# Two steps of the first chunk in float32 products: windowed attention with a gated MLP on one core

## The chip, the cores and the metric

The kernel runs on one core of a Trainium2 chip. The metric is the device time of one execution, in microseconds (us). A core has a matrix engine (PE, TensorE), three engines for elementwise work (ACT, ScalarE; DVE, VectorE; POOL, GpSimd), and queues that issue DMA transfers (SP's is the one used here for nearly all loads). Each engine runs its own instructions in the order in which the program lists them, and waits where an operand isn't there yet.

## The reference

Attention with a window of 128 keys and four sink keys, over 4 batches of 8 heads, 768 positions and 64 columns a head; its output, as 3072 rows of 512, goes through an MLP with 2048 hidden columns.

```
scores = q @ k.T / 8, kept where key < n_sink or 0 <= query - key < window
x = softmax(scores) @ v            # heads side by side: 3072 x 512
h = x @ w_in                       # 512 x 2048
g = h * tanh(softplus(h))
y = g @ w_out                      # 2048 x 512
```

## The kernel before, in words

The rows are cut into twelve chunks of 256. The first four, one of each batch, are worked alone (each has 8 steps of two hidden blocks of 128 columns); the other eight go in twos (16 steps of one hidden block). For each pair of heads the kernel makes scores (`att`, PE), mask and maximum (`p`, DVE), exponential (ACT), the division by the sum (L476 on DVE or L477 on ACT), transposes (L487, PE), a copy of them out of PSUM (`pth`, L292 or L295), and the product with the values (`outs`, L521), for two pairs of heads at a time in the first chunks. Its result is `x`, transposed.

A product of the MLP is made of float32r products, which keep fewer bits than float32. So each operand is split: a high part (`h`, a rounding copy) and a low part (`l`, the operand minus its high part), and a product takes three: high by high, high by low, low by high. `outs` makes the two parts of `x` (copy, then subtraction on DVE). `weights` makes the parts of a weight block: w_in and w_out come as 64-bit numbers, and s1 to s5 turn one into a float32 `z` and a rest `e`; then s7 copies the high part, s6 subtracts it from `z` and s8 adds `e`, which gives the low part. There are 32 such blocks. `step` does one hidden step: the first product into `hp` (L570), the gate in five operations on ACT and DVE (L580 to L587, in `u`), the split of `u` into `gh` and `gl`, and the second product into the accumulators (L609).

Nothing in this is ordered by hand alone. A planner gives every task a rank (the tables WI and WO for weight blocks, PAIRS for pairs of heads and `outs`), a modelled duration on each engine that may do it, and then places the tasks one after the other on the engine and at the place that it finds best; the program lists each engine's instructions in that order. Where the planner sees PE idle for over 250 ns ahead of a task with a new PSUM tile, or ahead of the first accumulators, it puts in filler products on zeros (`zero`, L771), which write nothing that is used. The tag `w` is a pool of 84 tiles of SBUF that weights, `x` and some temporaries share.

The three chunks 0 to 2 take turns, two steps of each at a time (PARTS, GROUP), and chunk 0 begins: so steps 0 and 1 of chunk 0 are the first work of the MLP, while the attention of the next chunks and the making of the weights go on.

Of the kernel before, what the change touches and what calls it, by code (L numbers as in the profile page):

```python
# [50 lines left out]
WO = -6.08, 3, 3.74, 4.03, 10.17, 6.19, 10.46, 11.32, 13.67, 15.66, 16.2, 9.12, 16.69, 18.91, 17.44, 17.26
PAIRS = (-17.41, -16.23, -9.53, -11.15, -11.81, -7.6, -8.1, -9, -4.69, -5.4, -6.04, -1.91, -3.65, -2.92, -0.58, -1.56,
         -1.55, 13.22, 16.4, 17.74, 20.65, 20.36, 19.52, 22, 21.07, 22.86, 25.11, 23.59, 26.75, 29.16, 28.34, 27.91, 30.86, 29.76, 29.47, 32.18, 32.77, 31.74, 36.46, 35.02,
         38.31, 42.01, 40.85, 41.2, 44.31, 42.85, 44.3, 47.22, 48.89, 48.43, 50.78, 51.16, 52.28, 54.74, 55, 55.47, 58.81, 60.67, 58.15, 62.94, 63.34, 61.48, 66.09, 66.95, 68.71, 71.34, 69.96, 73.76, 76.29, 76.39, 76.12, 79.36)
# [9 lines left out]
NEAR, SLOW = 2000, 4000  # L64
DUOS = (0, 1, 2, 3)
# [9 lines left out]
def f32(ap):  # L75
    return ap.bitcast(F32)
# [184 lines left out]
class Fast(Base):  # L261
# [55 lines left out]
    def weights(self, f, *ranks):  # L317
        nc, add = self.nc, self.plan.add
        deps = []
        for src, nm, r in zip((self.w_in, self.w_out), ("wi", "wo"), ranks):  # L320
# [3 lines left out]
            z.brief = e.brief = True  # L324
# [10 lines left out]
            s7 = add(r + .03, self.copy_ways(512, lambda hi=hi: hi.t, lambda z=z: f32(z.t)), [s3], [z], [hi])  # L335
# [173 lines left out]
    def outs(self, pairs, r, x, tag="att"):  # L509
# [33 lines left out]
    def step(self, st, f, rank, begins, ends, wdeps, last):  # L543
# [11 lines left out]
        eager = last and f >= st.steps - QUICK  # L555
        g1 = []
# [19 lines left out]
        u = Buf("u", [P, 2, T])  # L576
# [10 lines left out]
        e = add(r + .55, {DVE: (dve_t(N), lambda: nc.vector.scalar_tensor_tensor(u.t, u.t, 1.0, hp.t, ALU.subtract, ALU.mult))}, [a], [u, hp])  # L587
        gg = add(r + .57, self.copy_ways(N, lambda: gh.t, lambda: u.t), [e], [u], [gh])
# [105 lines left out]
    def run(self):  # L694
# [3 lines left out]
        self.wh, self.wl = ({"wi": [], "wo": []} for _ in range(2))  # L698
# [6 lines left out]
        for m, block in enumerate(blocks):  # L705
            wide = len(block) == 2
            st = SimpleNamespace(rows=[b * S + c3 * T for b, c3 in block], x_done=[{} for _ in block], part={}, kept=[], steps=NF if wide else NF // 2)
            st.x = [(Buf("w", [P, 2, T], F32R), Buf("w", [P, 2, T], F32R)) for _ in range(KT if wide else KT // 2)]
            pairs = []
            for pr in range(NPAIR):  # L710
# [7 lines left out]
                if wide or both:  # L718
                    rank, x = next(ranks), (*st.x[pr if wide else pr // 2], None, True)
                else:  # L720
                    rank, x = rank + unit * (TB + OVP + .05), (*st.x[pr // 2], pr % 2, pr % 2 == 0)
                done = self.outs(pairs, rank, x, BANKS["o"][turn] if turn < len(BANKS["o"]) else "att")
                for d in st.x_done:
                    d[pr] = done
                    if both:
                        d[pr - 1] = done
# [330 lines left out]
```

## Time and profile before

| what | value |
|---|---|
| median of 3 runs | 689.11 us (689.0 to 689.19) |
| the profiled execution's own time | 690.23 us |
| its span, first to last instruction | 688.4 us |
| PE busy | 679.2 us, 99% of the span |
| ACT busy | 525.4 us, 76% |
| DVE busy | 501.8 us, 73% |
| POOL busy | 124.4 us, 18% |
| mean granted clock of PE | 0.998 of full speed |

The profile is one execution. A share over the whole span says little by itself: the stretches differ in what limits them, and fillers and matmuls that wait a little inside the pipeline count as busy.

### The profile page before, as it was taken

The numbers are of one execution on the slowest core, as the hardware profiler recorded it, in microseconds if no ns is written. First come the engines' busy times: TensorE is split into PE (matmuls) and PEld (weight loads), VectorE is DVE, ScalarE is ACT, GpSimd is POOL, SyncE is SP. The second block draws the span as 40 slices with busy tenths as digits, with TensorE's granted clock in tenths as the row PEclk, the third lists the DMA queues.
The fourth block names the chain that finished last, engine by engine and source line by source line (L and its number), as shares of the span: only waits on it lengthen the run. The fifth ranks groups of instructions, "written<-read, shape, count | busy, mean of one in ns | idle before, by whom it ended". The sixth has DMA issues, their size and how long they took to land.

```text
span 688.4 us, 12130 instructions
## 1 busy us (share of the span) xinstructions
PE 679.2 (99%) x3980; PEld 563.6 (82%) x3980; DVE 501.8 (73%) x1442; ACT 525.4 (76%) x1223; POOL 124.4 (18%) x128
## 2 busy tenths in 40 slices
PE   8999999999999999999999999999999999999997
PEld 6778888988888888887888888887888787888885
DVE  8999999999896887666875886667677567432342
ACT  6999898987977876767876886778777676666672
POOL 1422321121104233120132131222010110000000
PEclk9999999999999999999999999999999999999999
DMA  6564343343535334041323331133340300010001
GB/s 211 175 185 124 123 139 114 116 135 98 161 97 156 88 83 134 16 110 39 95 79 91 112 86 55 40 86 95 101 109 1 86 0 25 1 62 0 1 0 67
DMA packets 49272, 60.20 MB, mean 87 GB/s; under 512 B 4912, under 2 KB 42160, under 8 KB 49200
## 3 DMA queue, kind: packets, MB, share of 16 engines
q1 hardware_dynamic: 48624, 57.69, 29.2%
q10 hardware_dynamic: 576, 1.64, 0.6%
q8 instruction: 34, 0.56, 0.3%
q14 instruction: 38, 0.31, 0.1%
HBM read 53.02 MB, written 6.29 MB: 86 GB/s over the span
## 4 chain that ended last, share of the span: by engine, by line
PE 84%; ACT 9%; DVE 5%; DMA 1%; issue 1%; ACTq 0%
PE hp L570 31%; PE acc L609 22%; PE att L609 12%; PE att L521 5%; PE att L445 5%; PE att L570 3%; ACT p L462 3%; PE att L487 2%; ACT p L477 1%; PE att L525 1%; ACT w L292 1%; ACT pth L292 1%; DMA raw<-w_in 1%; DVE u L587 1%; PE busy L1000 1%; ACT u L582 1%
## 5 line engine op out<-in xcount | busy, mean ns | idle before, releaser
L570 PE MATMUL hp<-w,w 128*128 128x256 f32 (+1 forms) x1440 | 269.8, 335 | 0.0
L570 PEld LDWEIGHTS hp<-w,w 128*128 128x128 f32 x1440 | 220.2, 189 | 28.3 <-issue 1.0
L609 PE MATMUL acc<-w,gh 128*128 128x512 f32 x500 | 137.9, 400 | 0.8 <-ACT w L292 0.5
L609 PEld LDWEIGHTS acc<-w,gh 128*128 128x128 f32 x500 | 87.7, 188 | 19.3 <-ACT gh L292 1.6
L462 ACT ACTIVATE p<-p,nm 128x136 f32<-128x136 f32 (+2 forms) x192 | 80.4, 428 | 21.2 <-DVE nm L459 20.6
L582 ACT ACTIVATE u<-u,bias 128x512 f32<-128x512 f32 x96 | 69.5, 724 | 35.0 <-DVE u L581 34.8
L587 DVE SCALAR_TENSOR_TENSOR u<-u,hp 128x512 f32<-128x512 f32 x88 | 60.1, 683 | 40.4 <-ACT u L586 37.8
L292 ACT ACTIVATE gh<-u 128x512 fp32r<-128x512 f32 x88 | 55.8, 634 | 33.7 <-DVE u L587 31.5
L580 ACT ACTIVATE u<-hp 128x512 f32<-128x512 f32 x88 | 52.5, 596 | 33.6 <-PE hp L570 32.0
L609 PE MATMUL acc<-w,gl 128*128 128x512 f32 x250 | 75.5, 394 | 0.0
L305 DVE TENSOR_TENSOR gl<-u,gh 128x512 fp32r<-128x512 f32 x72 | 51.8, 720 | 29.8 <-PE att L609 14.5
L584 ACT ACTIVATE u<-u,bias 128x512 f32<-128x512 f32 x96 | 69.6, 725 | 2.1
L303 POOL TENSOR_TENSOR w<-raw,w 64x400 fp32r<-64x400 f32 (+1 forms) x40 | 45.6, 1145 | 135.4 <-ACT w L292 50.9
L581 DVE TENSOR_SCALAR u<-u 128x512 f32<-128x512 f32 x96 | 43.0, 448 | 34.1 <-ACT u L580 33.7
L609 PE MATMUL att<-w,gh 128*128 128x512 f32 x244 | 67.5, 394 | 0.0
L586 ACT ACTIVATE u<-u 128x512 f32<-128x512 f32 x96 | 60.7, 632 | 1.9
L459 DVE CUSTOM_DVE_ANT_0 p<-att,m 128x136 f32<-128x136 f32 (+2 forms) x192 | 54.9, 313 | 3.1 <-PE att L442 1.2
L609 PEld LDWEIGHTS acc<-w,gl 128*128 128x128 f32 x250 | 46.2, 188 | 9.1 <-DVE gl L305 0.2
L457 DVE COPY_PREDICATED att<-behind,att 128x128 f32<-128x128 int32 x128 | 34.4, 292 | 25.6 <-PE att L445 25.0
L609 PEld LDWEIGHTS att<-w,gh 128*128 128x128 f32 x244 | 44.6, 188 | 8.8
L445 PEld LDWEIGHTS att<-w,w 128*128 128x128 f32 x256 | 41.1, 188 | 7.4 <-PE att L609 0.4
L445 PE MATMUL att<-w,w 128*128 128x264 f32 x256 | 45.8, 287 | 0.0
(115 smaller groups left out, 958.3 us busy)
## 6 DMA issues: line engine op xcount, KB each, us to landing
raw<-k_p SPq DMA_DIRECT2D x64, 200.0 KB, 3.4
raw<-q_p SPq DMA_DIRECT2D x64, 128.0 KB, 3.1
raw<-w_out SPq DMA_DIRECT2D x15, 512.0 KB, 3.6
raw<-w_in SPq DMA_DIRECT2D x14, 512.0 KB, 3.5
vt<-v_b SPq DMA_DIRECT2D x32, 192.0 KB, 2.6
y<-u SPq DMA_DIRECT2D x20, 256.0 KB, 2.1
ks<-k_p SPq DMA_DIRECT2D x16, 132.0 KB, 2.8
qh<-q_p SPq DMA_DIRECT2D x16, 128.0 KB, 2.9
```

Source lines behind the costliest of these rows:

```text
L292: ways[ACT] = act_t(n, psum), lambda: nc.scalar.activation(dst(), src(), AF.Copy, scale=scale or 1.0)
L305: way = dve_t(n), lambda: nc.vector.tensor_tensor(dst(), a(), b(), ALU.subtract)
L445: yield nc.tensor.matmul(st[e].t, part.t[:, e, cols], ks[e].t[:, c0:c0 + n], start=n_ == 0, stop=n_ == 1)
L459: a = add(r(.03 + .01 * e), {DVE: (dve_t(nw) + 8, lambda st=st, pv=pv, nm=nm, e=e, mask=mask, n=n, nw=nw: nc.vector.tensor_tensor_reduce(o ...
L462: a = add(r(.05 + .01 * e), {ACT: (act_t(nw, ptr=2), lambda pv=pv, nm=nm, i=i, e=e: nc.scalar.activation(pv(), pv(), AF.Exp, bias=nm.t[:, ...
L570: yield nc.tensor.matmul(out, w_.t[:, fs], x_, start=kt == 0 and n_ == 0, stop=kt == KT - 1 and n_ == 2)
L580: a = add(r + .5, {ACT: (act_t(N, True), lambda: nc.scalar.activation(u.t, hp.t, AF.Exp))}, g1, [hp], [u])
L582: sq = add(r + .52, {ACT: (act_t(N, ptr=1), lambda: nc.scalar.activation(u.t, u.t, AF.Square, bias=self.one)), DVE: shared((dve_t(N), lamb ...
L584: a = add(r + .53, {ACT: (act_t(N, ptr=1), lambda: nc.scalar.activation(u.t, u.t, AF.Ln, bias=self.half if sq.eng == ACT else self.one, sc ...
L586: a = add(r + .54, {ACT: (act_t(N), lambda: nc.scalar.activation(u.t, u.t, AF.Exp, scale=-1.0))}, [a], [u])
L587: e = add(r + .55, {DVE: (dve_t(N), lambda: nc.vector.scalar_tensor_tensor(u.t, u.t, 1.0, hp.t, ALU.subtract, ALU.mult))}, [a], [u, hp])
L609: yield nc.tensor.matmul(acc[at].t, g_.t[:, y, ts_], w_.t, start=new and n_ == 0, stop=done)
```

## The change

Chunk 0's steps 0 and 1 (`WHOLE = 2, 0, 0`) are made of single float32 products in place of three float32r products. For them `outs` copies chunk 0's result out of PSUM as a whole (`xw`), and makes the high and low part from that copy later (rank + XL), on ACT or DVE and on POOL or DVE; the later steps of chunk 0 still use the parts. Eight weight blocks (the first four of w_in and of w_out) are first completed as float32 (s6 now adds `e` to `z`), and their parts follow from the sum later (s7 copy, s8 subtraction, rank + HL). In the two steps `u` isn't split, so a copy to `gh` and a subtraction to `gl` each are gone, twice. All ranks (WI, WO, PAIRS) and some planner constants are new, and with them the order on every engine.

```diff
-PEN_C, PEN_S, PEN_N, PEN_J, PEN_Q = 50.59, 0, 2.67, 0, 3392.52
-WI = -8.52, -5.11, -2.45, -0.51, 7.12, 8.58, 9.74, 3.15, 12.1, 12.88, 13.09, 12.16, 13.77, 16.2, 17.29, 16.24
...
+PEN_C, PEN_S, PEN_N, PEN_J, PEN_Q = 50.59, 0, 9.82, 0, 2948.59
+WI = -11.75, -4.16, -4.06, -3.48, 7.63, 8.07, 7.38, 7.81, 11.31, 12.69, 13.76, 13.95, 17.17, 17.54, 17.59, 17.42
...
+WHOLE = 2, 0, 0
+XL, HL = 1.0, 1.0
...
             hi.users, lo.users = 1, 1
-            z.brief = e.brief = True
+            whole = f < 2 * max(WHOLE)
...
-            s7 = add(r + .03, self.copy_ways(512, lambda hi=hi: hi.t, lambda z=z: f32(z.t)), [s3], [z], [hi])
+            if not whole:
+                s7 = add(r + .03, self.copy_ways(512, lambda hi=hi: hi.t, lambda z=z: f32(z.t)), [s3], [z], [hi])
...
-            s6 = add(r + .06, self.sub_ways(512, lambda z=z: f32(z.t), lambda z=z: f32(z.t), lambda hi=hi: f32(hi.t)), [s7, s4], [z, hi])
-            s8 = add(r + .08, {
-                POOL: (pool_t(512), lambda z=z, e=e, lo=lo: nc.gpsimd.tensor_tensor(lo.t, f32(z.t), f32(e.t), ALU.add)),
-                DVE: shared((dve_t(512), lambda z=z, e=e, lo=lo: nc.vector.tensor_tensor(lo.t, f32(z.t), f32(e.t), ALU.add)), PEN_J)}, [s5, s6], [z, e], [lo])
+            if whole:
+                s6 = add(r + .06, {
+                    POOL: (pool_t(512), lambda z=z, e=e: nc.gpsimd.tensor_tensor(f32(z.t), f32(z.t), f32(e.t), ALU.add)),
+                    DVE: shared((dve_t(512), lambda z=z, e=e: nc.vector.tensor_tensor(f32(z.t), f32(z.t), f32(e.t), ALU.add)), PEN_J)}, [s5, s4], [z, e])
+                s7 = add(r + .07 + HL, self.copy_ways(512, lambda hi=hi: hi.t, lambda z=z: f32(z.t)), [s6], [z], [hi])
+                s8 = add(r + .08 + HL, self.sub_ways(512, lambda lo=lo: lo.t, lambda z=z: f32(z.t), lambda hi=hi: f32(hi.t)), [s7], [z, hi], [lo])
+                self.ww[nm].append((z, s6))
+            else:
+                s6 = add(r + .06, self.sub_ways(512, lambda z=z: f32(z.t), lambda z=z: f32(z.t), lambda hi=hi: f32(hi.t)), [s7, s4], [z, hi])
+                s8 = add(r + .08, {
+                    POOL: (pool_t(512), lambda z=z, e=e, lo=lo: nc.gpsimd.tensor_tensor(lo.t, f32(z.t), f32(e.t), ALU.add)),
+                    DVE: shared((dve_t(512), lambda z=z, e=e, lo=lo: nc.vector.tensor_tensor(lo.t, f32(z.t), f32(e.t), ALU.add)), PEN_J)}, [s5, s6], [z, e], [lo])
...
-        h, l, k, newx = x
+        h, l, k, newx, xw = x
         at = (lambda z: z.t) if k is None else lambda z: z.t[:, k:k + 1, :]
+        if xw:
+            w = add(r + .1, self.copy_ways(n * T, lambda: at(xw), lambda: o.t, True), [a], [o] + ([] if newx else [xw]), [xw] if newx else [])
+            a = add(r + .1 + XL, self.copy_ways(n * T, lambda: at(h), lambda: at(xw)), [w], [xw] + ([] if newx else [h]), [h] if newx else [])
+            c = add(r + .12 + XL, self.sub_ways(n * T, lambda: at(l), lambda: at(xw), lambda: f32(at(h))), [a],
+                    [xw, h] + ([] if newx else [l]), [l] if newx else [])
+            return [a, c], [w]
         a = add(r + .1, self.copy_ways(n * T, lambda: at(h), lambda: o.t, True), [a], [o] + ([] if newx else [h]), [h] if newx else [])
         c = add(r + .12, self.sub_ways(n * T, lambda: at(l), lambda: o.t, lambda: f32(at(h)), (DVE,)), [a],
                 [o, h] + ([] if newx else [l]), [l] if newx else [])
-        return [a, c]
+        return [a, c], []
...
+                        if whole:
+                            yield nc.tensor.matmul(hp.t[:, y, :], f32(wiw[f1][0].t[:, fs]), st.xw[kh].t[:, kt % 2, :], start=kt == 0, stop=kt == KT - 1)
+                            continue
...
+                if whole:
+                    g1.append(add(r + .1 + .1 * y + .05 * kh, {PE: (whole_t(T, T), first)},
+                                  [t for pr in (2 * kh, 2 * kh + 1) for t in st.w_done[pr]] + [wiw[f1][1]] + g1[-1:],
+                                  [st.xw[kh], wiw[f1][0]] + ([] if fr else [hp]), [hp] if fr else []))
+                    continue
...
-        u = Buf("u", [P, 2, T])
+        u = Buf("w" if whole else "u", [P, 2, T])
...
+        if whole:
+            jobs = [(y, t) for y in range(2) for t in range(TB)]
+            for y, t in jobs:
+                f1, new = 2 * f + y, begins and y == 0
+
+                def product(f1=f1, y=y, t=t, new=new, done=ends and y == 1):
+                    yield nc.tensor.matmul(acc[t].t, u.t[:, y, t * P:(t + 1) * P], f32(wow[f1][0].t), start=new, stop=done)
+                st.tail = add(rank + 1.45 + .1 * y + .05 * t, {PE: (whole_t(512), product)}, [e, st.tail, wow[f1][1]],
+                              [u, wow[f1][0]] + ([] if new else [acc[t]]), [acc[t]] if new else [])
+                if ends and y == 1:
+                    self.store(st, rank, t, False, last)
+            return
```

What this does to the order, at three places. First ACT, where the first block of chunk 0's attention result (`att`, written by `outs`) is copied out of PSUM; `w` tiles are the copies, `p` and `rc` belong to the softmax, `pth` to the transposes. Before:

```order
L477 ACTIVATE p_72_0_331<-p_72_0_331,rc_0_392 128x128
L477 ACTIVATE p_72_0_331<-p_72_0_331,rc_0_392 128x256
L292 ACTIVATE w_0_422<-att_0_374 128x512
L292 ACTIVATE pth_0_429<-att_0_407 128x2x128
L477 ACTIVATE p_78_0_352<-p_78_0_352,rc_0_405 128x128 x2
L477 ACTIVATE p_78_0_352<-p_78_0_352,rc_0_405 128x256 x2
```

After the change:

```order
L298 ACTIVATE w_0_396<-att_0_369 128x512
L493 ACTIVATE p_71_0_329<-p_71_0_329,rc_0_388 128x128
L298 ACTIVATE w_0_416<-w_0_396 128x512
L346 ACTIVATE raw_66<-raw_66 128x512
L334 ACTIVATE w_0_429<-raw_67 128x512
```

Before, the copy in the third row is the high part, and DVE subtracts from `att` for the low part. Now the first row is the copy as a whole, and the third row makes the high part from it.

Second PE, in the first products of chunk 0 (`hp`): the operand after the arrow is `x` (422, 432, 522, 528 before; 396, 524 now), the second one the weights; `att` and `acc` rows are attention of later chunks. Before, from the first half of the second step on:

```order
L570 MATMUL hp_0_610<-w_0_422,w_0_492 128x256
L570 MATMUL hp_0_610<-w_0_432,w_0_492 128x256
L570 MATMUL hp_0_610<-w_0_422,w_0_536 128x256
L570 MATMUL hp_0_610<-w_0_422,w_0_492 128x256
L570 MATMUL hp_0_610<-w_0_432,w_0_492 128x256
L570 MATMUL hp_0_610<-w_0_422,w_0_536 128x256
L487 MATMUL acc_187<-ident,p_141_0_480 128x128 x2
L487 MATMUL acc_0_626<-ident,p_141_0_480 128x128 x4
L442 MATMUL att_0_636<-ks_60,qh_62 128x256
L442 MATMUL att_1_637<-ks_60,qh_62 128x256
```

After the change, from the end of the last fillers on:

```order
L589 MATMUL hp_0_402<-w_0_524,w_0_198 128x256 x2
L503 MATMUL acc_187<-ident,p_131_0_451 128x128 x2
L589 MATMUL hp_0_402<-w_0_396,w_0_250 128x256 x2
L503 MATMUL acc_0_567<-ident,p_131_0_451 128x128 x4
L503 MATMUL att_0_576<-ident,p_140_0_472 128x128 x2
L503 MATMUL att_0_579<-ident,p_140_0_472 128x128 x4
L458 MATMUL att_0_587<-ks_60,qh_62 128x128
L458 MATMUL att_1_588<-ks_60,qh_62 128x128
L589 MATMUL hp_0_402<-w_0_524,w_0_250 128x256 x2
L458 MATMUL att_0_605<-ks_61,qh_63 128x128
L458 MATMUL att_1_606<-ks_61,qh_63 128x128
```

Six products of a half step (three for each of two blocks of 128 rows of weights) have become two, and the order of the attention among them is another. Ahead of the first of these rows stand the last fillers of the changed program; it has 61 fillers in all, and the program before has 75, of which the last 15 stand behind the first products of both steps.

Third PE, at the first of the second products (`acc<-w,gh` before, `acc<-w,w` now, where the last name is `u`). Before:

```order
L609 MATMUL acc_0_824<-w_0_309,gh_0_799 128x512
L609 MATMUL acc_0_824<-w_0_368,gh_0_799 128x512
L609 MATMUL acc_0_834<-w_0_309,gh_0_799 128x512
L609 MATMUL acc_0_834<-w_0_368,gh_0_799 128x512
L521 MATMUL att_0_840<-pth_0_784,vt_65 64x256 x2
L521 MATMUL att_0_840<-pth_0_784,vt_65 64x128 x2
L521 MATMUL att_0_840<-pth_0_740,vt_64 64x256 x2
L521 MATMUL att_0_840<-pth_0_740,vt_64 64x128 x2
L609 MATMUL acc_0_824<-w_0_606,gh_0_799 128x512
L609 MATMUL acc_0_824<-w_0_723,gh_0_799 128x512
L609 MATMUL acc_0_834<-w_0_606,gh_0_799 128x512
L609 MATMUL acc_0_834<-w_0_723,gh_0_799 128x512
```

After the change:

```order
L503 MATMUL att_0_724<-ident,p_210_0_615 128x128 x2
L503 MATMUL att_0_728<-ident,p_210_0_615 128x128 x4
L627 MATMUL acc_0_737<-w_0_231,w_0_619 128x512
L458 MATMUL att_0_747<-ks_60,qh_62 128x256
L458 MATMUL att_1_748<-ks_60,qh_62 128x256
L458 MATMUL att_0_753<-ks_61,qh_63 128x256
L458 MATMUL att_1_754<-ks_61,qh_63 128x256
L627 MATMUL acc_0_766<-w_0_231,w_0_619 128x512
L537 MATMUL att_0_777<-pth_0_734,vt_65 64x256 x2
L537 MATMUL att_0_777<-pth_0_734,vt_65 64x128 x2
L537 MATMUL att_0_777<-pth_0_697,vt_64 64x256 x2
L537 MATMUL att_0_777<-pth_0_697,vt_64 64x128 x2
```

Four products of high parts in a row, with the low ones behind them, have become single products between attention rows. In all 48 products L570 of 256 columns and 24 products L609 of 512 columns are replaced by 16 and 8.

## Rows read from the trace of the kernel before

**Rows 1.** The chain of waits: shares of the span by engine.

```profile
PE 84%; ACT 9%; DVE 5%; DMA 1%; issue 1%; ACTq 0%
```

**Rows 2.** Windows: us; busy of PE, PEld, DVE, ACT, POOL; clock, DMA share, GB/s.

```profile
28.40:44.20 15.80, 15.34 (x125) 12.06 (x122) 15.07 (x57) 15.80 (x51) 4.47 (x4) 1.00 0.63 183
44.20:106.00 61.80, 61.29 (x420) 52.09 (x418) 57.94 (x151) 58.16 (x138) 15.60 (x12) 1.00 0.46 136
```

**Rows 3.** Windows: the ninth and the sum of nine PE gaps, and two later ones.

```profile
27.67:28.38 0.71, 0.71 (x10) 0.71 (x9) 0.68 (x2) 0.71 (x4) 0.71 (x2) 1.00 0.28 73
sum 7.91, PE 6.64 PEld 5.16 DVE 7.71 ACT 7.87 POOL 1.26; mean PE 0.74 PEld 0.57 DVE 0.86 ACT 0.87 POOL 0.14
...
39.89:40.28 0.39, 0.39 (x6) 0.38 (x5) 0.39 (x2) 0.39 (x2) 0.00 (x0) 1.00 0.58 135
41.32:42.83 1.51, 1.12 (x13) 1.14 (x12) 1.44 (x9) 1.51 (x6) 0.00 (x0) 1.00 0.96 358
```

**Rows 4.** Timeline of ACT: start, us, instruction, idle before it.

```profile
7.11 0.40 ACT L462 ACTIVATE p<-p,nm 128x128 f32<-128x128 f32 x1 [4.69 <-DVE nm L459]
...
20.53 0.80 ACT L477 ACTIVATE p<-p,rc 128x128 f32<-128x128 f32 x2
21.24 0.58 ACT L292 ACTIVATE w<-att 128x512 fp32r<-128x512 f32 x1
21.71 0.37 ACT L292 ACTIVATE pth<-att 128x256 f32<-128x256 f32 x1
21.98 1.48 ACT L477 ACTIVATE p<-p,rc 128x128 f32<-128x128 f32 x4
23.36 0.62 ACT L292 ACTIVATE w<-w 128x512 fp32r<-128x512 f32 x1
23.88 0.39 ACT L462 ACTIVATE p<-p,nm 128x128 f32<-128x128 f32 x1
...
24.27 0.39 ACT L462 ACTIVATE p<-p,nm 128x128 f32<-128x128 f32 x1
...
25.99 0.68 ACT L327 ACTIVATE w<-raw 128x512 f32<-128x512 f32 x1
26.57 0.69 ACT L338 ACTIVATE raw<-raw 128x512 f32<-128x512 uint32 x1
27.13 0.51 ACT L462 ACTIVATE p<-p,nm 128x256 f32<-128x256 f32 x1
...
27.63 0.51 ACT L462 ACTIVATE p<-p,nm 128x256 f32<-128x256 f32 x1
...
34.51 0.63 ACT L580 ACTIVATE u<-hp 128x512 f32<-128x512 f32 x1
```

**Rows 5.** Windows of L570 alone: first, last and sum of its first six windows.

```profile
22.55:23.36 0.81, 0.81 (x6) 0.76 (x6) 1.00 0.00 0
...
38.02:39.55 1.53, 1.53 (x12) 1.48 (x12) 1.00 0.81 297
sum 6.64, PE 6.63 PEld 6.09; mean PE 1.11 PEld 1.01
```

**Rows 6.** Windows of L609 alone: the sum of its first seven windows.

```profile
sum 6.11, PE 6.10 PEld 4.08; mean PE 0.87 PEld 0.58
```

**Rows 7.** Groups of PE by shape: busy us, mean ns of one, idle before.

```profile
L570 PE MATMUL hp<-w,w 128*128 128x512 f32 x672 | 167.5, 393 | 0.0
...
L570 PE MATMUL hp<-w,w 128*128 128x256 f32 x768 | 102.4, 285 | 0.0
...
L521 PE MATMUL att<-pth,vt 128*64 128x256 f32 x192 | 30.1, 392 | 0.6 <-DVE nm L459 0.3 <-issue 0.2
L521 PE MATMUL att<-pth,vt 128*64 128x128 f32 x320 | 25.7, 273 | 0.0
```

**Rows 8.** Group of DVE: the subtraction for the low part of `u`.

```profile
L305 DVE TENSOR_TENSOR gl<-u,gh 128x512 fp32r<-128x512 f32 x72 | 51.8, 720 | 29.8 <-PE att L609 14.5 <-ACT gh L292 10.1 <-ACT u L580 4.1
```

**Rows 9.** Timeline of PE, one row near 106 us.

```profile
106.21 2.15 PE L609 MATMUL acc<-w,gh 128*128 128x512 f32 x8 [0.51 <-ACT w L292]
```

More of the change, by code (lines that the diff above doesn't have):

```diff
@@ L47 @@
 W1 = P + SK
-PEN_C, PEN_S, PEN_N, PEN_J, PEN_Q = 50.59, 0, 2.67, 0, 3392.52
-OTP, OVP = 1.29, 1.53
-WI = -8.52, -5.11, -2.45, -0.51, 7.12, 8.58, 9.74, 3.15, 12.1, 12.88, 13.09, 12.16, 13.77, 16.2, 17.29, 16.24
[L51 to L54, printed above, removed]
+PEN_C, PEN_S, PEN_N, PEN_J, PEN_Q = 50.59, 0, 9.82, 0, 2948.59
+OTP, OVP = 1.29, 1.66
+WI = -11.75, -4.16, -4.06, -3.48, 7.63, 8.07, 7.38, 7.81, 11.31, 12.69, 13.76, 13.95, 17.17, 17.54, 17.59, 17.42
+WO = -8.77, 0.93, 7.24, -2.07, 8.58, 8.49, 8.63, 8.63, 13.02, 7.48, 16.01, 8.46, 14.11, 17.3, 18.94, 17.76
+PAIRS = (-16.2, -16.07, -9.7, -11.02, -11.38, -6.77, -8.73, -8.16, -4.19, -5.17, -5.86, -2.31, -3.75, -3.59, -0.92, -1.98,
+         0.09, 5.58, 14.12, 13.78, 18.97, 18.78, 15.35, 22.58, 22.3, 22.25, 24.1, 23.7, 24.54, 26.36, 26.58, 26.67, 28.8, 28.49, 28.59, 30.35, 30, 32.04, 34.2, 34.3,
+         34.15, 36.54, 37.48, 37.34, 40.44, 41.76, 39.9, 45.97, 44.51, 45.92, 47.8, 49.29, 47.43, 52.79, 52.97, 51.48, 56.89, 55.88, 57.66, 59.77, 60.31, 58.98, 64.51, 65.37, 64.16, 68.46, 68.95, 70.52, 72.6, 73.62, 72.2, 79.65)
 GROUP = 3
 PARTS = 2, 2, 2, 2
-UNITS = 1.109, 0.975, 0.905, 0.7
-SPL = 0.52
+UNITS = 1.109, 0.975, 1.023, 0.7
+SPL = 0.62
 BLOCKS = 1, 1, 1, 1, 2, 2, 2, 2
@@ L93, in pool_t, with whole_t @@
     return 149 + 2.15 * n
+def whole_t(*ns):
+    return sum(n / .6 + 30 for n in ns)
 def pe_t(*ns):
@@ L323, in weights @@
             hi.users, lo.users = 1, 1
-            z.brief = e.brief = True
+            whole = f < 2 * max(WHOLE)
+            z.brief, e.brief = not whole, True
             ld = self.load(r - 1.0, raw, lambda raw=raw: raw.t.rearrange("p n t -> p (n t)"), src[f].bitcast(I32), 512)
@@ L555, in step @@
         eager = last and f >= st.steps - QUICK
+        whole = f < st.whole
+        if whole:
+            (wiw, wow) = (self.ww[nm] for nm in ("wi", "wo"))
         g1 = []
@@ L587, in step @@
         e = add(r + .55, {DVE: (dve_t(N), lambda: nc.vector.scalar_tensor_tensor(u.t, u.t, 1.0, hp.t, ALU.subtract, ALU.mult))}, [a], [u, hp])
+        if whole:
+            jobs = [(y, t) for y in range(2) for t in range(TB)]
[8 more added lines that the diff above has]
+            return
         gg = add(r + .57, self.copy_ways(N, lambda: gh.t, lambda: u.t), [e], [u], [gh])
@@ L697, in run @@
         chunks = sorted(((b, c3) for b in range(B) for c3 in range(NCH)), key=lambda z: (z[1] > 0, z))
-        self.wh, self.wl = ({"wi": [], "wo": []} for _ in range(2))
+        self.wh, self.wl, self.ww = ({"wi": [], "wo": []} for _ in range(3))
         wdeps = [self.weights(f, WI[f], WO[f]) for f in range(NF)]
@@ L706, in run @@
             wide = len(block) == 2
-            st = SimpleNamespace(rows=[b * S + c3 * T for b, c3 in block], x_done=[{} for _ in block], part={}, kept=[], steps=NF if wide else NF // 2)
+            st = SimpleNamespace(rows=[b * S + c3 * T for b, c3 in block], x_done=[{} for _ in block], w_done={}, part={}, kept=[], steps=NF if wide else NF // 2)
             st.x = [(Buf("w", [P, 2, T], F32R), Buf("w", [P, 2, T], F32R)) for _ in range(KT if wide else KT // 2)]
+            whole = m < len(WHOLE) and WHOLE[m]
+            st.whole, st.xw = whole, [Buf("w", [P, 2, T]) if whole else None for _ in st.x]
             pairs = []
@@ L718, in run @@
                 if wide or both:
-                    rank, x = next(ranks), (*st.x[pr if wide else pr // 2], None, True)
+                    rank, x = next(ranks), (*st.x[pr if wide else pr // 2], None, True, st.xw[pr if wide else pr // 2])
                 else:
[L721 to L724, printed above, removed]
+                    rank, x = rank + unit * (TB + OVP + .05), (*st.x[pr // 2], pr % 2, pr % 2 == 0, st.xw[pr // 2])
+                done, w = self.outs(pairs, rank, x, BANKS["o"][turn] if turn < len(BANKS["o"]) else "att")
+                for d, z in [(st.w_done, w), *((d, done) for d in st.x_done)]:
+                    d[pr] = z
                     if both:
-                        d[pr - 1] = done
+                        d[pr - 1] = z
                 pairs = []
```

## The prediction

> **What bounds the kernel now.** I read the chain of waits first: PE holds 84% of it, ACT and DVE nearly all the rest [rows 1]. So the time is PE's work plus the time in which PE has none. The shares by stretch say where that is. From 28.4 to 44.2 us ACT is busy for all of 15.80 us and DVE for 15.07 [rows 2]: in the start the attention, the making of the weights and the gate fill these two, and PE waits for them. From 44.2 to 106 PE is busy for 61.29 of 61.80, with ACT (58.16) and DVE (57.94) close behind [rows 2]; later on PE is alone. The reader should see that a product saved or added late costs its full length, while one in the start may fall into a gap.
>
> The timeline of PE shows the gaps: runs of fillers with some idle time, each counted from its start to the next other product. Nine of them, up to 28.38 us, hold 7.91 us; two more, at 39.89 and 41.32, hold 0.39 and 1.51 [rows 3]. Behind 42.83 there is no filler, and the next idle time of size is 0.51 us at 106.21 [rows 9]. So 9.81 us are what the start could give back at most, and much of that lies ahead of the first `x`, where there is nothing to do.
>
> **The products.** The two steps lose 48 products of 256 columns and 24 of 512. The first stand in six windows of 6.64 us together [rows 5], the second in seven of 6.11 us [rows 6]: 12.75 us. For the float32 products the trace of before has near relatives, the products with the values (L521): the program has 96 of 256 and 160 of 128 columns, the trace 192 and 320 records, so one product is two records. A record of 256 columns takes 392 ns and one of 128 columns 273, that is 119 ns for 128 columns; between float32r records of 512 and 256 columns lie 393 - 285 = 108 ns for 256 [rows 7]. At the full clock of 2.4 GHz (granted 1.00 in these stretches [rows 2]) a float32r record takes one cycle a column, about 0.42 ns, and a float32 record two. L521 uses half the array for each head, so its two heads may overlap; the new products fill the array and can't. So a product takes 4 cycles a column: 0.427 us for 256 columns, 0.853 for 512. Sixteen and eight of them take 13.65 us.
>
> That is bare column time, and the removed ones had more than theirs: 48 x 256 + 24 x 512 = 24576 columns are 10.24 us, so 2.51 were extra. Within a run the extra is small: twelve records in 1.53 us against six in 0.81 [rows 5] are 0.12 us a record, 0.013 over its columns; for 72 records 0.96. The other 1.55 falls on the entry into a piece between other work; the products stood in 11 such pieces, so 0.14 each. The new ones stand in 12 pieces: 1.69. I take 13.65 + 1.69 = 15.34, so **+2.6 us** of PE work. Bounds: without entries +0.9; with 0.013 on each of 48 records +3.2.
>
> The Trainium skill ("FP8 and Floating Point Precision", section "TensorE Precision Notes") says that true float32 takes four passes through the array; that speaks against the change, which puts them in place of three products. The rows agree with four. By the page alone, with every pass at bare column time, my estimate would be a third more than 10.24, so +3.4 in place of +2.6.
>
> **The gaps of the start.** ACT sets them: from its first exponential at 7.11 it runs without a break. I add spacings, start to next start [rows 4]: 0.39 for an exponential of 128 columns with its read of the sum, 0.50 for 256, 0.58 for s1 of a weight block, 0.56 for its rest (raw<-raw), 0.35 for a division, 0.52 for a copy of 512 columns in SBUF, 0.47 and 0.27 for copies of 512 and 256 from PSUM. As a check, ACT's queue ahead of the first gate exponential holds 14, 12, 5, 4, 14, 5, 4 and 5 of these and a small one: 27.4 us, so 34.5 us; it started at 34.51 [rows 4]. In the changed order the copy of the second block of `x` stands behind 12, 12, 4, 3, 5, 4, 4 and 4: 21.5 us; with the copy's own 0.58 it is done at 29.2. PE's second piece of first products waits for it, and this is where the last of the 61 fillers stand. Before, PE came to the same place, with the same attention behind it, at 28.38. One float32 piece (0.85 + 0.14) is behind it in place of six products (0.81). So the gaps are 7.91 + 0.82 - 0.18 = 8.55 us, and then nothing is planned where 1.90 stood: **-1.3 us** against 9.81. Bounds: -1.8 if the gaps shrink with the number of fillers (14 of 75 fewer, of 9.81), 0 if PE still runs dry where the two late gaps were.
>
> **ACT, DVE and the queues.** Two copies for `gh` go and two for the parts of `x` come: nothing. Two subtractions for `gl` go, 0.72 each [rows 8]: 1.4 us less on DVE. The weight blocks need as many operations as before, in another order; s7 and s8 move one rank back, behind the first products that no longer need them. They hold their `w` tiles longer, of which there are 84. SP's queue lists its first loads in the same order, so the blocks land as before. Of the 1.4 us, anything from 0 to all comes back between 44 and 106 us, where three engines are full at once; I take **-0.5**. The stall of 0.51 us at 106 is a matter of order; gone or not, half: **-0.25**.
>
> **The sum** is +2.6 - 1.3 - 0.5 - 0.25 = +0.55, on the profiled execution's 690.23 us: 690.8. The runs shown have their median 1.12 lower, at 689.11, so I predict 689.7 us. A difference of 0.2% (1.4 us) is about what a measurement of this kernel tells from no change.
>
> **The rivals.**
> - *The start gives back more.* The entries cost the float32 products nothing (+0.9), the gaps shrink by 1.8, DVE's 1.4 and the stall's 0.51 all come back: -2.8, so 686.3 us. For it: DVE and ACT are full up to 60 us, and each us that they save lets PE start earlier. Against it: the first `x` comes no earlier by ACT's queue.
> - *A new wait at the second products* (the side of slower). L627 stands right behind the transposes, and four scores and a product with the values stand behind it on PE. If `u` is late there, all of them wait, and ACT and DVE for them. Its gate goes through ACT's full queue five times over, as it does now behind the gap of 1.51. Price: up to that gap once more, +0.55 + 1.5 = +2.05, so 691.2; from a delay of 0.85 on it decides. Against it: PE has 3 us more to do by then.
> - *Four passes at full price.* If entries weigh on float32 products as the in-run extra does on the others, the work is +3.4 and the sum +1.35: 690.5, on the edge. For it: two records a product, each with a weight load.
> - *The change is cheaper than it looks*: if the two records of a product overlap in the full array as the heads of L521 may, 6.8 us go, 683 us. Against it: the slopes, and that overlap needs free rows or columns.
>
> **The numbers.** Forecast within 0.2%: 0.46; more from the start 0.24; the new wait 0.17; the full price 0.10, half of it beyond the bound; cheap products 0.03. So faster 0.27, same 0.51, slower 0.22. The range from 687.0 to 691.3 takes in most of the first rival and the second, and leaves out cheap products and the ends.
>
> **What would show it.** Right: 16 products L589 of two records at 0.43 us each and 8 at 0.85 (L627), no filler behind 30 us, PE at the second half of the first products near 29.2 us, gaps of 8.5 us, DVE free of two subtractions. Wrong: idle time of PE at L627 or L654 (the new wait), a resumption before 28 or behind 30 us, a granted clock below 1.00 in the start, or stretches behind 200 us that differ by over 1 us, which nothing here explains.

## The result: slower by 1.15%, and the profile after

The changed kernel takes 697.65 us (median of 4 runs, 696.52 to 698.8), the one before 689.15 beside it: a ratio of 1.0115, with a 95% interval of 1.0096 to 1.0134. The prediction was 689.7, with a range up to 691.3. The profiled execution took 696.52 us, with a span of 694.7 (before 690.23 and 688.4), so 6.3 us of span are to be explained.

The page of the changed kernel, its busy row for the engines and its chain of waits:

```profile
PE 680.6 (98%) x3942; PEld 559.2 (80%) x3942; DVE 499.4 (72%) x1451; ACT 522.2 (75%) x1208; POOL 134.2 (19%) x132
...
PE 72%; DVE 11%; ACT 11%; issue 3%; DMA 2%; POOL 0%; DVEq 0%; POOLq 0%; ACTq 0%
```

PE's share of the chain fell from 84% [rows 1] to 72%, and DVE's and ACT's rose: PE waits for them at more places. The two stretches of [rows 2], now:

```profile
28.40:44.20 15.80, 15.31 (x102) 11.02 (x100) 14.49 (x56) 15.80 (x50) 5.21 (x6) 1.00 0.51 160
44.20:106.00 61.80, 61.37 (x400) 49.14 (x399) 59.39 (x157) 60.14 (x144) 16.85 (x13) 1.00 0.49 150
```

They hardly differ. The new products, in windows from the start of a piece to the next other product (the first of seven pieces of L589 and their sum, then the first of five of L627 and theirs; us, PE's busy time and records, clock, DMA share, GB/s), which answer to [rows 5, 6]:

```profile
21.14:22.11 0.97, 0.97 (x4) 1.00 0.79 227
...
sum 7.72, PE 7.71; mean PE 1.10
```

```profile
43.74:44.70 0.96, 0.95 (x2) 1.00 0.40 43
...
sum 6.88, PE 6.87; mean PE 1.37
```

Together 14.60 us, where 12.75 stood and 15.34 were predicted. The gaps with fillers or idle time, windows as in [rows 3], the second, the last and the sum of nine:

```profile
8.64:12.48 3.84, 1.90 (x20) 1.00 0.77 219
...
27.84:29.62 1.78, 1.32 (x14) 1.00 0.88 275
sum 10.34, PE 7.01; mean PE 0.78
```

So the second piece of first products starts at 29.62 us (predicted 29.2), and no filler follows it, as predicted; but the gaps before it hold 10.34 us, more than the 9.81 of before.

**Where the 6.3 us arise.** PE's last product ends at 687.76 us (685.46 + 2.30); before at 683.34. The rest of the span is 6.94 us, before 5.06. So 4.4 us were lost up to PE's end and 1.9 behind it. To place the 4.4 I took the start of every run of products from the timeline of PE, less the sum of all products ahead of it in the program's order at their unhindered spacing (0.119 us for a float32r record of 256 columns, 0.227 for 512, 0.12 for scores and fillers, four cycles a column for float32, and so on). The difference, the lag, grows only where PE waits, also where it waits less than a product stays in the pipeline and the trace calls it busy. Means over stretches of 20 us of work (the work as a whole is 0.84 us more after; where float32 products stand, their bare time is in the work):

```
from us of work:    60    100    160    200    220    240    280    360    480    580
before           24.57  27.74  34.25  38.21  40.76  42.24  44.98  52.13  60.66  64.55
after            25.72  27.38  33.69  38.84  41.66  45.01  49.57  56.37  65.41  67.96
late_ranks_back  25.44  27.10  33.59  37.96  40.48  41.86  44.72  51.67  60.15  64.07
```

With the 0.84 us of work added, the changed kernel is 2.0 us behind at 60 us of work, 0.5 at 100 and 0.3 at 160; then it loses 4 to 5 us between 160 and 300 us of work (194 to 351 us of the span; how much exactly depends on the spacing at which attention's products are counted), and is 4.3 behind at the end. The waits of PE that the profile names between 200 and 500 us (engine, waits for, total, times, longest):

```profile
PE att L520 <- DVE pth L511: 0.9, 1, 0.9
PE acc L654 <- ACT gh L298: 0.3, 1, 0.3
PE att L503 <- DVE pth L511: 0.2, 1, 0.2
```

The windows say the same: from 260 to 280 us PE works on 117 records before, in all of 20.00 us, and on 99 in the changed kernel, in 18.80 us. Before, then after:

```profile
260.00:280.00 20.00, 20.00 (x117) 16.52 (x116) 14.79 (x49) 15.27 (x40) 4.86 (x8) 1.00 0.40 114
...
260.00:280.00 20.00, 18.80 (x99) 15.43 (x98) 16.68 (x43) 15.85 (x39) 1.80 (x2) 1.00 0.48 128
```

### The profile page after: what moved, and what is told of

Its sections match the earlier page's. It is cut to its first block, busy times and chain, and to the rows that moved or that the text cites. A ratio compares the mean times of both kernels' runs of the same rounds, so it can differ in the third digit from the quotient of the medians.

```text
span 694.7 us, 12056 instructions
## 1 busy us (share of the span) xinstructions
PE 680.6 (98%) x3942; PEld 559.2 (80%) x3942; DVE 499.4 (72%) x1451; ACT 522.2 (75%) x1208; POOL 134.2 (19%) x132
## 4 chain that ended last, share of the span: by engine, by line
PE 72%; DVE 11%; ACT 11%; issue 3%; DMA 2%; POOL 0%; DVEq 0%; POOLq 0%; ACTq 0%
PE hp L598 25%; PE acc L654 16%; PE att L654 11%; PE att L537 5%; PE att L461 4%; PE att L598 3%; PE att L503 2%; ACT p L478 2%; DVE w L311 2%; ACT w L298 1%; DVE u L620 1%; PE hp L589 1%; DVE u L614 1%; ACT u L615 1%; ACT gh L298 1%
## 5 line engine op out<-in xcount | busy, mean ns | idle before, releaser
L598 PE MATMUL hp<-w,w 128*128 128x256 f32 (+1 forms) x1392 | 265.0, 338 | 0.4 <-DVE u L620 0.2
L598 PEld LDWEIGHTS hp<-w,w 128*128 128x128 f32 x1392 | 214.5, 189 | 30.0 <-issue 1.8
L654 PE MATMUL acc<-w,gh 128*128 128x512 f32 x484 | 132.1, 397 | 0.4 <-ACT gh L298 0.3
L654 PEld LDWEIGHTS acc<-w,gh 128*128 128x128 f32 x484 | 85.5, 188 | 16.0 <-ACT gh L298 1.0
L615 ACT ACTIVATE u<-u,bias 128x512 f32<-128x512 f32 x94 | 67.8, 721 | 33.3 <-DVE u L614 33.0
L309 POOL TENSOR_TENSOR w<-raw,w 64x400 fp32r<-64x400 f32 (+1 forms) x44 | 49.3, 1125 | 139.8 <-ACT w L298 53.1
L311 DVE TENSOR_TENSOR gl<-u,gh 128x512 fp32r<-128x512 f32 x67 | 47.7, 712 | 36.0 <-PE att L654 19.9
L654 PE MATMUL acc<-w,gl 128*128 128x512 f32 x242 | 72.5, 393 | 0.0
L614 DVE TENSOR_SCALAR u<-u 128x512 f32<-128x512 f32 x94 | 43.9, 467 | 39.0 <-ACT u L613 38.6
L617 ACT ACTIVATE u<-u,bias 128x512 f32<-128x512 f32 x94 | 67.7, 720 | 2.1
L654 PE MATMUL att<-w,gh 128*128 128x512 f32 x244 | 68.4, 396 | 0.0
L654 PEld LDWEIGHTS att<-w,gh 128*128 128x128 f32 x244 | 44.3, 189 | 8.6 <-DVE pth L511 0.2
L654 PEld LDWEIGHTS acc<-w,gl 128*128 128x128 f32 x242 | 44.6, 188 | 8.3
L309 POOL TENSOR_TENSOR gl<-u,gh 128x512 fp32r<-128x512 f32 x24 | 31.5, 1314 | 87.7 <-PE att L654 28.4
L511 DVE TENSOR_TENSOR pth<-att,tri 128x512 f32<-128x512 f32 x64 | 42.7, 686 | 5.3 <-PE att L503 5.1
```

The lines of the kernel that those rows point to most:

```text
L309: ways[POOL] = pool_t(n), lambda: nc.gpsimd.tensor_tensor(dst(), a(), b(), ALU.subtract)
L311: way = dve_t(n), lambda: nc.vector.tensor_tensor(dst(), a(), b(), ALU.subtract)
L615: sq = add(r + .52, {ACT: (act_t(N, ptr=1), lambda: nc.scalar.activation(u.t, u.t, AF.Square, bias=self.one)), DVE: shared((dve_t(N), lamb ...
L617: a = add(r + .53, {ACT: (act_t(N, ptr=1), lambda: nc.scalar.activation(u.t, u.t, AF.Ln, bias=self.half if sq.eng == ACT else self.one, sc ...
L654: yield nc.tensor.matmul(acc[at].t, g_.t[:, y, ts_], w_.t, start=new and n_ == 0, stop=done)
```

## The experiments

Three theories stood at first. A: the new ranks of the later blocks put their attention in an order in which PE waits. B: the float32 products and the parts made later cost it. C: any order but the one before meets new waits, at no fixed place. Ranks are counted from 1 here; 1 to 24 of PAIRS belong to the four single chunks, 25 to 36 to the fifth block (the first of two chunks), 37 to 48 to the sixth, 49 to 72 to the last two. (The labels count blocks from 0.) `NEW` and `OLD` are the tables of the changed kernel and of the one before.

| kernel | median, us | ratio to before (95%) | PE's last product | from there to the end |
|---|---|---|---|---|
| before | 689.15 | | 683.34 | 5.06 |
| after | 697.65 | 1.0115 (1.0096 to 1.0134) | 687.76 | 6.94 |
| new_ranks_only | 698.29 | 1.0128 (1.0112 to 1.0143) | 688.76 | 7.54 |
| float32_old_ranks | 694.88 | 1.0069 (1.0056 to 1.0083) | 688.83 | 5.27 |
| late_ranks_back | 690.86 | 1.0020 (1.0011 to 1.0029) | 683.80 | 5.20 |
| late_ranks_alone | 698.00 | 1.0120 (1.0105 to 1.0134) | 688.41 | 7.49 |
| block4_ranks_alone | 691.84 | 1.0024 (1.0015 to 1.0033) | 684.86 | 5.44 |
| block4_ranks_kept | 691.37 | 1.0020 (1.0009 to 1.0031) | 685.34 | 5.16 |
| blocks67_ranks_back | 696.53 | 1.0091 (1.0077 to 1.0105) | 687.31 | 6.89 |
| blocks45_ranks_alone | 696.49 | 1.0089 (1.0074 to 1.0105) | 686.49 | 7.21 |
| nine_of_block5_back | 691.28 | 1.0025 (1.0016 to 1.0035) | 683.83 | 5.57 |
| six_of_block5_back | 693.67 | 1.0048 (1.0033 to 1.0062) | 685.71 | 5.19 |
| late_ranks_1p5_later | 698.14 | 1.0112 (1.0097 to 1.0128) | 689.01 | 8.29 |
| late_ranks_1_earlier | 690.58 | 1.0006 (0.9997 to 1.0015) | 682.86 | 5.04 |
| three_ranks_1p5_later | 697.57 | 1.0117 (1.0100 to 1.0134) | 686.69 | 7.31 |
| early_ranks_no_float32 | 692.99 | 1.0038 (1.0025 to 1.0051) | 685.90 | 5.30 |
| one_float32_step | 693.60 | 1.0061 (1.0044 to 1.0078) | 686.38 | 5.02 |
| stores_split | 694.61 | 1.0064 (1.0052 to 1.0076) | 688.06 | 6.24 |
| late_ranks_alone_split | 695.94 | 1.0092 (1.0076 to 1.0109) | 687.84 | 5.46 |
| back_and_1_earlier | 693.71 | 1.0059 (1.0047 to 1.0071) | 686.65 | 4.75 |

The two columns at the right are of one profiled execution each; a median of the kernel before in the same series was 689.4 to 690.1, so medians of different series compare to within 1 us only.

### Which part of the change

`new_ranks_only` (`-WHOLE = 2, 0, 0`, `+WHOLE = 0, 0, 0` in the changed kernel):

> The new constants and ranks, with no float32 product (all first-chunk steps as three float32r products again, as before the change). Theory A (the new ranks and planner constants put the work of the later blocks in an order in which TensorE waits between 210 and 330 us, some 3.5 us, and the end is 1.9 us longer; the float32 products themselves cost about nothing): 694 to 697 us, with a PE wait for DVE or ACT of 0.3 us or more somewhere between 210 and 330 us. Theory B (the float32 products and the parts made later cause it): 688.5 to 690 us. Theory C (any order other than the one before meets new waits of some us, at no fixed place): 691 to 700 us, with the waits elsewhere.

`float32_old_ranks`, the changed kernel with the numbers of before:

```diff
-PAIRS, WI, WO, PEN_N, PEN_Q, OVP, UNITS, SPL = NEW
+PAIRS, WI, WO, PEN_N, PEN_Q, OVP, UNITS, SPL = OLD
```

> The float32 products of the first chunk's two steps with the constants and ranks of before. Theory A (late order of the new ranks): 689 to 690.5 us, the sum of the prediction without its change of the start. Theory B (the float32 products themselves): 696 to 699 us. Theory C (any other order meets new waits): 691 to 697 us, with waits of PE at places that the changed kernel does not have.

`late_ranks_back` (the changed kernel) and `late_ranks_alone` (the kernel before):

```diff
-PAIRS = NEW
+PAIRS = NEW[:24] + OLD[24:]
...
-PAIRS = OLD
+PAIRS = OLD[:24] + NEW[24:]
```

> The changed kernel with the ranks of the four late blocks (the last 48 of PAIRS) as before; the first 24, the weights' ranks, the planner's constants and the float32 products stay changed. Theory A: the waits between 210 and 330 us go, 692 to 694.5 us (697.65 less 3.5, and less 1.9 more if the end follows them). Theory B: 697 to 698 us. Theory C: anything from 692 to 700 us, with waits at other places.

> The kernel before with the last 48 ranks of PAIRS of the changed kernel and nothing else. Theory A: 692 to 695 us, with PE waits between 210 and 330 us. Theory B: 688.5 to 690 us. Theory C: 691 to 697 us, with waits at other places.

The new numbers lose as much without a float32 product (698.29), so B falls as the main cause. Putting the late ranks back gave more than theory A had asked for (690.86, under its 692), and the late ranks alone cost more (698.00, above its 695). The last 48 ranks alone cost the kernel before 8.6 us by the medians of that series (698.00 against 689.38), and putting them back in the changed kernel gives 6.8 us of its 8.5 back: theory A, with the end 1.7 us shorter too. `late_ranks_back` has the same products and as many fillers as the changed kernel, so its row in the table of lags is the plain comparison: they run together up to 160 us of work and differ by 4.9 at 280. Its windows, against those of after:

```profile
260.00:280.00 20.00, 20.00 (x115) 16.44 (x114) 14.92 (x50) 14.78 (x39) 4.99 (x8) 1.00 0.39 114
```

`float32_old_ranks` bears C out in part: with the ranks of before the float32 products cost 5.5 us, PE has 85 fillers (61 in the changed kernel, 75 before), and its last product comes at 688.83. The early numbers of the change fit its products; the late ones are what loses.

### Which of the late ranks

`block4_ranks_alone`, `blocks45_ranks_alone` (the kernel before with NEW ranks 25 to 36, and 25 to 48), `block4_ranks_kept`, `blocks67_ranks_back` (the changed kernel with OLD ranks 37 to 72, and 49 to 72):

```diff
+PAIRS = OLD[:24] + NEW[24:36] + OLD[36:]
...
+PAIRS = OLD[:24] + NEW[24:48] + OLD[48:]
...
+PAIRS = NEW[:36] + OLD[36:]
...
+PAIRS = NEW[:48] + OLD[48:]
```

> The kernel before with only ranks 25 to 36 of PAIRS (the fifth block, the first wide one) as in the changed kernel. If these twelve ranks make the loss that the last 48 made (8.6 us): 696 to 698 us, with PE waits between 200 and 340 us and a long end. If the three later blocks make it: 689 to 690.5 us. If it is shared: 691 to 695 us.

> The changed kernel with ranks 37 to 72 of PAIRS (the last three blocks) as before, ranks 25 to 36 left as changed. If the fifth block's ranks make the loss: 696 to 698 us. If the three later blocks make it: 690.5 to 691.5 us, as with all 48 put back. If it is shared: 692 to 695 us.

> The changed kernel with ranks 49 to 72 of PAIRS (the last two blocks) as before; ranks 37 to 48 stay changed. Those of 37 to 48 are the ones whose attention falls between 240 and 340 us, where PE falls behind: if they make the loss, 695 to 698 us. If the last two blocks make it, 690.5 to 692 us.

> The kernel before with ranks 25 to 48 of PAIRS as changed, the last 24 as before. If ranks 37 to 48 make the loss: 694 to 698 us. If the last two blocks make it: 691 to 692.5 us, as with ranks 25 to 36 alone.

Twelve ranks, 37 to 48, part the four kernels: with the new ones 696.5 on either base, with the old ones 691.4 and 691.8. I had set the fifth block first, since its steps run there; it is the attention of the sixth, done during those steps, that counts. Within the twelve:

```diff
+PAIRS = NEW[:39] + OLD[39:]
...
+PAIRS = NEW[:42] + OLD[42:]
```

> The changed kernel with ranks 40 to 72 of PAIRS as before; of the sixth block's twelve only the first pair of heads (ranks 37 to 39) stays changed. With ranks 37 to 48 all changed and 49 to 72 back the time was 696.53, with all of 37 to 72 back 691.37. If the loss starts with the first pair's loads and splits: 695 to 696.5 us; if it lies in the nine others: 691 to 692 us; if each pair adds its share: 692 to 694 us.

> The changed kernel with ranks 43 to 72 of PAIRS as before; the first two pairs of heads of the sixth block (ranks 37 to 42) stay changed. TensorE's waits at 271.9 and 277.4 us stand beside the splits of this block's k and q on DVE: if these two pairs make them, 695 to 697 us; if the last two pairs make the loss, 691 to 692.5 us.

Ranks 37 to 39 cost nothing: PE's end is 683.83, as with all put back (683.80). With 40 to 42 changed too, the loss between 260 and 280 us is there in full, and the wait with it. But the time, 693.67, lies between the two ranges that were expected. Above the kernel before in each series, the excess is 1.3 us with 37 to 39 changed, 3.7 with 37 to 42, 6.4 with 37 to 48 and 8.5 with 37 to 72: ranks 40 to 42 make 2.4 us, 43 to 48 another 2.7 (1.7 of them in the end of the span, 6.89 against 5.19 us), 49 to 72 the last 2.1. Window, then wait of PE, of `six_of_block5_back`:

```profile
260.00:280.00 20.00, 18.67 (x99) 15.33 (x98) 16.75 (x43) 15.73 (x39) 1.95 (x2) 1.00 0.49 128
```

```profile
PE att L520 <- ACT u L615: 1.0, 1, 1.0
```

This is what stands there in the changed kernel (timeline: start, us, instruction, idle before it):

```profile
268.11 1.42 DVE L311 TENSOR_TENSOR w<-raw,w 128x512 fp32r<-128x512 f32 x1 [0.45 <-ACT w L298]
...
269.20 0.58 ACT L613 ACTIVATE u<-hp 128x512 f32<-128x512 f32 x1
...
269.85 0.57 DVE L311 TENSOR_TENSOR w<-raw,w 64x400 fp32r<-64x400 f32 x1
270.45 0.43 DVE L614 TENSOR_SCALAR u<-u 128x512 f32<-128x512 f32 x1
...
270.91 1.30 DVE L311 TENSOR_TENSOR w<-raw,w 64x400 fp32r<-64x400 f32 x2
...
275.08 1.19 PE L654 MATMUL acc<-w,gh 128*128 128x512 f32 x4 [0.28 <-ACT gh L298]
...
277.26 0.38 PE L503 MATMUL att<-ident,p 128*128 128x128 f32 x2
277.40 0.48 PE L654 MATMUL acc<-w,gl 128*128 128x512 f32 x1
...
277.97 1.28 DVE L511 TENSOR_TENSOR pth<-att,tri 128x512 f32<-128x512 f32 x2
...
278.80 0.30 PE L520 MATMUL att<-ident,ks 128*128 128x128 f32 x1 [0.92 <-DVE pth L511]
```

DVE splits k and q of pairs to come (L311 on `raw`) between the operations of the first wide step's gate: ACT's `u` is done at 269.78, and DVE goes on with it (L614) at 270.45, behind a split. The gate's product L654 waits 0.28 us at 275.08; that the splits make this wait is argued from the order, not shown. The last transposes (L503, 277.26) and the transpose of the sink columns (L520) have one product between them, and L520 waits for DVE's `pth`. It is the same wait in `six_of_block5_back`, though the profile names ACT there: in both L520 starts 0.83 us behind DVE's L511, in that kernel at 279.06. With the late ranks put back, six products of the MLP stand between the same two, and neither waits:

```profile
279.93 0.60 PE L503 MATMUL att<-ident,p 128*128 128x128 f32 x4
280.29 1.62 PE L598 MATMUL hp<-w,w 128*128 128x512 f32 x6
281.75 0.27 PE L520 MATMUL att<-ident,ks 128*128 128x128 f32 x1
```

### Too early, or in another order

The new ranks 37 to 72 are lower by 2.7 on average.

```diff
+PAIRS = NEW[:36] + [x + 1.5 for x in NEW[36:]]
...
+PAIRS = OLD[:36] + [x - 1.0 for x in OLD[36:]]
...
+PAIRS = NEW[:39] + [x + 1.5 for x in NEW[39:42]] + NEW[42:]
```

> The changed kernel with 1.5 added to each of ranks 37 to 72 (their order among themselves as changed, but all placed a step and a half later; against before they stand 2.7 steps earlier on average). If the loss comes from attention being placed too early, where it crowds the steps between 200 and 340 us: 693 to 695.5 us, and fewer attention exponentials between 200 and 320 us than the 97 of the changed kernel (78 before). If it comes from the order of the pieces among themselves: 697 to 698 us.

> The kernel before with 1.0 taken from each of ranks 37 to 72. If attention placed earlier is what costs: 691 to 693 us. If the order of the pieces among themselves costs: 689 to 690 us, as before.

> The changed kernel with 1.5 added to ranks 40 to 42 of PAIRS alone (the second pair of heads of the sixth block: 34.3, 34.15 and 36.54). If these three, placed too early for DVE and ACT at the start of the first wide block, make the PE fall behind between 260 and 300 us: the waits at 271.9 and 277.4 us shrink and the last product of TensorE comes 1.5 to 3 us earlier, 694.5 to 696.2 us (the end stays long). If they only lose in any order but the one before: 697 to 699 us.

By the times the order is the better account: a shift of all late ranks by a step costs the kernel before nothing clear of the noise (+0.5 us), and 1.5 steps don't help the changed one; 690.58 and 698.14 both lie a little outside the ranges for it. The traces are less plain. With all 1.5 later, 88 records of attention exponentials stand between 200 and 320 us (97 after, 78 before; two records each), the lag at 280 us of work is 47.55 in place of 49.57, and PE then waits for DVE's `u` near the end:

```profile
609.47 1.67 PE L598 MATMUL hp<-w,w 128*128 128x512 f32 x6 [2.13 <-DVE u L620]
```

With three ranks later, PE is busy for all of 260 to 280 us, the wait is gone, and PE's last product comes 1.07 us earlier in the profiled execution, the fastest of its four by 1.7 us; the median is the same. The end is 7.31 us there, and PE has 69 fillers in place of 61. So those three ranks make the wait that was named, and taking it away alone doesn't bring the time back.

### The float32 products themselves

Both with `PAIRS = NEW[:24] + OLD[24:]` and the other new numbers, with `WHOLE = 0, 0, 0` and `WHOLE = 1, 0, 0`:

> The last 48 ranks as before and no float32 product; the constants, the weights' ranks and the first 24 ranks stay changed. It tells what the float32 products themselves cost beside these ranks: by the prediction's own terms (2.6 us more PE work, 0.5 us less for DVE, some of the idle start given back) 689 to 690.5 us against 690.86 with them; if the float32 products are what gives the start back, 691.5 to 694 us; if they only cost their PE work, 688 to 688.5 us.

> The last 48 ranks as before, and the first chunk's first step alone in float32 (the second step as three float32r products). Half of the 2.6 us of PE work is gone: 689.3 to 690.5 us if PE work alone counts; 691 us or more if the order that the ranks give is made for two such steps and the loss or gain comes from what waits, not from the work.

With two float32 steps these ranks give 690.86, with none 692.99, with one 693.60; above the kernel before in their own series that is 1.5, 2.9 and 3.6 us. Beside these ranks the products are worth some 1.5 us, beside those of before they cost 5.5: the price belongs to the pair of them, and half of the change isn't half of the effect.

### The end of the span

Leaving out the two kernels below, the end from PE's last product is 6.9 to 8.3 us in seven kernels of the table and 4.8 to 5.6 in eleven, and SyncE's records in the trace are 529 to 533 in the seven and 535 to 543 in the eleven. So I lengthened SyncE's list, in the changed kernel by eight stores (which stand between 179 and 276 us) and in `late_ranks_alone` by twelve:

```diff
-nc.sync.dma_start(self.out[row:row + P, :], ot.t)
+for z in range(2):
+    cols = slice(z * DM // 2, (z + 1) * DM // 2)
+    nc.sync.dma_start(self.out[row:row + P, cols], ot.t[:, cols])
```

> The changed kernel with its first eight stores of results issued as two of half the columns each (between 100 and 330 us; every other instruction in the same order). The long end (6.9 us from TensorE's last product to the end of the span, against 5.1 before) came in every kernel whose SyncE has 529 to 533 instructions in the trace, and in none with 539 or more, with two more fetches on the instruction queue q14; this brings it to some 542. If SyncE's length sets the end: 695.5 to 696 us and an end of 5.0 to 5.4 us. If the end follows from the late ranks in another way: 697 to 698 us and an end of 6.9.

> The kernel before with the last 48 ranks as changed (698.0 us, 529 instructions of SyncE, an end of 7.5 us), with twelve of its result stores issued as two of half the columns each, to some 541 instructions of SyncE; nothing else in the order differs. If SyncE's length sets the end: 694.5 to 696 us, as the eight split stores took 3.0 us from the changed kernel, and an end of 5.0 to 6.3 us. If not: 697.5 to 698.5 us.

The times fall by 3.0 and 2.1 us (3.9 and 2.6 above the kernel before in each series), with PE's last product about where it was (688.06 and 687.84 against 687.76 and 688.41). The end of the second goes from 7.49 to 5.46 us, and the packets of instructions on queue q14 from 684 us on from 9 to 7; the row of `late_ranks_alone`, then that of its split copy:

```profile
q14 instruction: 9, 0.07, 1.7%
```

```profile
q14 instruction: 7, 0.06, 1.1%
```

In the first the profiled execution, the longest of six, has an end of 6.24, more than expected: SyncE's wait for the last stores took 3.77 us there, 2.69 in the changed kernel. The ends of the other five aren't on record. That the length of SyncE's list sets some 2 us of the end is shown by the second.

SyncE's own records show where these 2 us lie. At the end of the program SyncE waits for its last stores and then goes through a closing list of semaphore waits. In each of the seven kernels with the long end it stands still a second time within that list, for 1.60 to 2.23 us, and always ahead of its record 523, though five different pairs of semaphores are waited for at that place in the seven (2.08 us in the changed kernel, up to 693.55 us). In the other thirteen, the two with split stores among them, record 523 comes no later than the wait for the last stores, and there is no such pause. What SyncE waits for at record 523, a fetch of instructions or something else, isn't shown.

### A version to beat both

```diff
+PAIRS = NEW[:24] + OLD[24:36] + [x - 1.0 for x in OLD[36:]]
```

> The changed kernel with ranks 25 to 36 of PAIRS as before and ranks 37 to 72 as before less 1.0. The late ranks put back gave 690.86, and the kernel before with this shift 690.58, its last product 0.5 us earlier. If the order of the later blocks counts by its own waits, whatever stands ahead of them: 690 to 690.6 us. If each order meets its own waits: 691 to 694 us.

The shift that cost the kernel before nothing clear of the noise costs 2 to 3 us here (693.71 against 690.86; 3.7 against 1.5 above the kernel before in each series). No version was faster than the kernel before.

## Why the prediction was wrong

**The step that failed** is what the sum leaves out: it has no term behind 106 us. The text knew that all ranks were new, priced their effect once ("a matter of order", -0.25), and put down stretches behind 200 us that differ by over 1 us as something "which nothing here explains". There they differ by some 4 us, and the end by 1.9. The cause is the late ranks of PAIRS, by the runs that put them back: 37 to 48 make 5.1 us of the 8.5 and 49 to 72 another 2.1. Some 2 us of this are SyncE's pause at its record 523; for the rest one wait of PE is shown (40 to 42, at L520), and which others make up the remainder stays open. None of the four rivals held this; the one on the side of slower looked for a late `u` at L627, where PE shows no wait.

**The part that was worked out** can be read from `late_ranks_back`, the change without the late ranks: 690.86, which is 1.5 us over 689.38 in its series (interval 0.8 to 2.0), against +0.55 predicted, so the sum was about 1 us short even there; its last product is 0.46 us later than before. Its terms were off in both directions:
- *The products*: +2.6 predicted, +1.85 measured (14.60 - 12.75). Four cycles a column hold; the entry was mis-sized, 0.08 us in place of 0.14 ((14.60 - 13.65) / 12). The Trainium skill ("FP8 and Floating Point Precision", section "TensorE Precision Notes") has four passes for true float32, and the rows agree: 0.48 us for a product of 256 columns (7.72 / 16), where four cycles a column at 2.4 GHz are 0.427. My estimate by that page, +3.4, was too high.
- *The gaps of the start*: -1.3 predicted, +0.5 measured (10.34 - 9.81). ACT's queue gave the place of the second piece well (29.62 for 29.2), but the gaps ahead of it grew: the sum took them over from before unchanged, and they hold 8.56 us without the last, against 7.20. Nor do the blocks land as before: SyncE issues the first load of w_out at 25.14 us, before at 23.03.
- *DVE's subtractions and the stall at 106 us*: -0.75 predicted together; the lag falls from +2.0 to +0.5 between 60 and 100 us of work, so about -1.5. The stall of 0.51 us at 106 us is gone. How much of it each has isn't shown.

So the sum was within 1 us for the part that it covered, and that by luck: its errors of size offset each other.

## What to carry to other kernels

Where a change replaces the table that orders the whole program, cost the new order along the whole span, not only where the edited operations stand; a few ranks hundreds of microseconds away can outweigh the edit. Split such a change early into the edit and the numbers, and those by stages; here one run with the last 48 of the 72 ranks put back told where 6.8 of 8.5 us were. Read PE's lag from the starts of its products, since most of a spread loss stands in no idle row: of the 4 us only 1.4 stand as idle time between 200 and 500 us, the rest in waits that the trace counts as busy.

## What I had not expected of the hardware

The end of the span isn't a constant. From PE's last product, with the same last stores, it was 4.8 to 5.6 us in twelve kernels and 6.9 to 8.3 in seven, by whether SyncE's list had 535 or more records or 533 or fewer (and 6.24 in one execution of `stores_split`), and splitting stores some 300 us or more ahead of the end took 2 us off it, by way of a pause of SyncE of 1.60 to 2.23 us at its record 523. The Trainium skill ("Runtime: NRT & Kernel Launch", section "The ~15µs preamble/postamble breakdown") lists the stages behind a kernel as fixed times (about 1.5, 1.5 and 2 us) and has instruction fetch run by itself. The pause lies ahead of those stages, in the program's own closing list (L1100 in the changed kernel), for which that section gives no time; the rows here show 9 packets of instructions on q14 from 684 us on with the pause and 7 without it.
